# QK steps in groups of two across unit borders, PV in the spare PSUM banks, column-tiled sums from unit 3 on

## The chip, the cores and the metric

One core of a Trainium2 chip. The metric is device time in microseconds (us) of one execution. Engines: TensorE (PE in the profile, PEld its weight loads), VectorE (DVE), ScalarE (ACT), GpSimd (POOL), and SyncE (SP), which issues most DMAs. Runs were timed in several rounds; the kernel before was timed in each, and its median there was 436.7 to 437.2.

## The reference

Attention with RMS-normalised queries and keys (8 batches, 12 heads, 448 tokens, head size 64), then a two-layer MLP over all tokens (768 to 2048 to 768) with a leaky ReLU:

```python
q_n, k_n = rmsnorm(q, g_q), rmsnorm(k, g_k)
attn = softmax(q_n @ k_n.T / sqrt(64))          # with the row maximum taken off
x = (attn @ v).transpose(0, 2, 1, 3).reshape(3584, 768)
h = x @ w_in
out = maximum(0.01 * h, h) @ w_out
```

## The kernel before

Four heads of one batch are a **unit** `u` (24 units, three to a batch). A unit has seven QK **steps**; a step is four 64x64-tiled matmuls that fill one **slot** (two PSUM banks; there are two slots), and one exponential on ScalarE empties it. The other four banks rotate as `aux` among everything else. PV is the product of the exponentials with the values (28 tiled matmuls a unit), `zcol` the sums by which it is divided. A step's maximum over all its rows (VectorE), a diagonal `dg`, a broadcast matmul into `pb` and two short VectorE steps give the shift `eb` of the unit's exponentials. MLP work of the batch before is cut into jobs (`moe1`: 6 matmuls of 448 columns, evacuated by ScalarE; `moe2`: 8 matmuls of 384 columns, every second one evacuated by VectorE) and dealt out between the QK groups.

```python
STEPS = ((0,), (1, 2), (3, 4), (5, 6))          # four groups a unit

def fed(u, d):                                   # a batch is complete here
    return u % NQ == 0 and d == 3

def fill(u, d, jobs):                            # deals the queue out evenly up to the next feeding
    total = sum(c for c, _ in queue)
    ...                                          # left: the weights up to fed(...), unit 3 excluded
    debt[0] += total * WD[d] / left
    while queue and debt[0] >= queue[0][0] * 0.5:
        c, fn = queue.pop(0); fn(); debt[0] -= c
        if jobs: jobs.pop(0)()
    for job in jobs: job()
...
push_moe1(0); push_moe2(0)                       # prologue: batch 0 is queued here
...
for u in range(3, NU):
    for d in range(4):
        qk(u, STEPS[d])
        if d == 0:
            shift_max(u)
            pv_slot(u - 1); zcol(u - 1)          # PV takes the second slot
            shift_mm(u)
            pv_out(u - 1); zcol_sum(u - 1)
        ex(u)
        ...
        if fed(u, d) and u > 3:                  # not for unit 3: batch 0 is queued already
            push_moe1(u // NQ - 1); push_moe2(u // NQ - 1)
        ...
            if d == 1: ...job(prep_ssq, u + 2, ALL, (ti,))       # sums of squares
            if d == 2:
                job(prep_rinv, u + 2)
                for ti in range(2):                              # queries, then keys
                    job(prep_norm, u + 2, ALL, (ti,))            # VectorE, 1.1 us each
                job(prep_trd, u + 2)                             # DMA transpose
        fill(u, d, jobs)                         # d == 3 has no VectorE preparation
```

(shortened; `...` marks cuts)

## Time and profile before

| what | value | from |
|---|---|---|
| time | 436.72 us (436.13 to 436.79, 3 runs) | timed runs |
| TensorE busy, clock granted | 96%, 0.995 | page, run |
| ScalarE, VectorE, GpSimd busy | 71%, 49%, 34% | page |
| idle of TensorE from 100 to 390 us | 0 | table of stretches |

The profiled execution of this kernel took 438.52 us, 1.8 more than the median of the timed ones. The prediction below shows the chain and the stretches. First the groups of instructions for the two MLP layers (line, engine, operation, shapes, count, busy time and mean), which count the work:

```profile
L350 PE MATMUL op<-wout,gt 128*128 128x384 f16 x896 | 153.6, 326 | 0.0
L329 PE MATMUL hps<-xt,win 128*128 128x448 f16 x756 | 151.0, 353 | 0.0
```

896 is 112 second-layer jobs of 8, and 756 is 126 first-layer jobs of 6 (two more ran in the prologue): each batch once. Then VectorE around the start of a unit (start, length, what, idle before it in brackets):

```profile
209.32 1.09 DVE L151 TENSOR_TENSOR n<-qg,rinv 128x896 f16<-128x896 f32 x1 [6.96 <-issue]
210.33 1.08 DVE L151 TENSOR_TENSOR n<-rk,rinv 128x896 f16<-128x896 f32 x1
214.42 1.10 DVE L216 TENSOR_REDUCE sT<-sT 128x1 f32<-128x896 f32 x1 [3.01 <-PE sT L179]
```

The two normalising multiplications (L151) are done 3 us before the next unit's maximum (L216): VectorE waits for TensorE there, not the other way round. In the whole run TensorE waited 2.0 us for the diagonal.

### The profile page before, as it was taken

The page shows a single profiled execution, that of the slowest core. Times are in us where ns is not written, and L with a number is a line of the kernel's source. Part 1 is how long each engine was busy: PE and PEld are TensorE (multiplying, and loading weights), DVE is VectorE, ACT ScalarE, POOL GpSimd, SP SyncE. Part 2 cuts the span into 40 slices and gives each one's busy share as a digit, 9 for nine tenths or more (in the row PEclk, how much of TensorE's full clock was granted, in tenths as well). Part 3 has the DMA queues.
Part 4 walks back from the last instruction along what each step waited for, and adds up shares of the span by engine and source line. Part 5 has one row for each costly group of instructions (what it writes and reads, how often), then busy time and mean ns, then how long its engine had stood idle before and what let it go on. Part 6 is the DMA issues. An engine that isn't in the chain of part 4 may idle for free.

```text
span 436.7 us, 8782 instructions
## 1 busy us (share of the span) xinstructions
PE 419.2 (96%) x3700; PEld 216.3 (50%) x3700; DVE 214.8 (49%) x319; ACT 309.5 (71%) x458; POOL 148.9 (34%) x102
## 2 busy tenths in 40 slices
PE   7788998999999999999999999999999999999995
PEld 6545443444455544554445544554445544555563
DVE  5887564874535744554445745555345612220021
ACT  6989887688976699877876699867877486534300
POOL 4987566533422432532330422532430110100000
PEclk9989999999999999999999999999999999999999
DMA  8999999689458856569447875779524630311022
GB/s 276 220 257 249 235 189 192 182 198 208 91 143 144 216 152 125 129 200 204 85 128 146 203 177 102 148 205 184 108 44 107 134 75 2 78 38 38 0 74 72
DMA packets 67980, 62.83 MB, mean 144 GB/s; under 512 B 37477, under 2 KB 62821, under 8 KB 67941
## 3 DMA queue, kind: packets, MB, share of 16 engines
q1 hardware_dynamic: 57664, 50.47, 46.7%
q0 software_dynamic: 10272, 11.80, 17.6%
q8 instruction: 29, 0.48, 0.4%
q14 instruction: 11, 0.08, 0.1%
q10 hardware_dynamic: 4, 0.00, 0.0%
HBM read 45.61 MB, written 11.01 MB: 130 GB/s over the span
## 4 chain that ended last, share of the span: by engine, by line
PE 83%; ACT 6%; DVE 5%; DMA 3%; issue 1%; DVEq 0%; ACTq 0%
PE op L350 32%; PE hps L329 31%; PE sT L179 8%; PE sT L314 5%; ACT et L198 4%; DMA qkT<-n 3%; PE zc L260 3%; DVE n L151 2%; PE sT L243 1%; PE pb L228 1%; PE warm L412 1%; DVE ssq L139 1%; DVE sT L216 0%; ACT rz L301 0%; ACT rz L300 0%
## 5 line engine op out<-in xcount | busy, mean ns | idle before, releaser
L198 ACT ACTIVATE et<-sT,eb 128x896 f16<-128x896 f32 x166 | 158.8, 1005 | 47.8 <-PE sT L179 35.7
L350 PE MATMUL op<-wout,gt 128*128 128x384 f16 x896 | 153.6, 326 | 0.0
L329 PE MATMUL hps<-xt,win 128*128 128x448 f16 x756 | 151.0, 353 | 0.0
L350 PEld LDWEIGHTS <-gt 128*128 128x128 f16 x896 | 84.7, 98 | 65.3 <-issue 12.1
L329 PEld LDWEIGHTS <-win 128*128 128x128 f16 x756 | 70.9, 98 | 71.3 <-issue 7.2
L294 POOL TENSOR_TENSOR xt<-x,rz 128x896 f16<-128x896 f32 x19 | 41.0, 2156 | 185.9 <-DMA rz<-zs 170.6
L331 ACT ACTIVATE gt<-hps 128x448 f16<-128x448 f32 x126 | 67.7, 544 | 21.3 <-PE hps L329 20.2
L354 DVE COPY ost<-op 128x384 f32<-128x384 f32 x56 | 31.1, 556 | 99.4 <-PE op L350 96.2
L134 POOL TENSOR_TENSOR qg<-rq,ggb 128x896 f32<-128x896 f32 (+2 forms) x25 | 61.3, 2454 | 36.7 <-DVE n L151 32.3
L179 PE MATMUL sT<-qkT 64*64 64x448 f16 x664 | 52.2, 364 | 6.4 <-ACT et L198 4.3
L151 DVE TENSOR_TENSOR n<-qg,rinv 128x896 f16<-128x896 f32 (+2 forms) x25 | 27.5, 1102 | 54.3 <-issue 26.7
L139 DVE TENSOR_REDUCE ssq<-sq 128x14 f32<-128x896 f32 (+2 forms) x49 | 50.0, 1053 | 1.1 <-ACT sq L126 1.1
L216 DVE TENSOR_REDUCE sT<-sT 128x1 f32<-128x896 f32 x22 | 24.1, 1093 | 31.9 <-PE sT L179 31.7
L179 PEld LDWEIGHTS <-qkT 64*64 64x64 f16 x672 | 15.4, 104 | 40.3 <-issue 35.0
L151 DVE TENSOR_TENSOR n<-rk,rinv 128x896 f16<-128x896 f32 (+2 forms) x25 | 33.6, 1348 | 0.0
L272 ACT COPY x<-sT 128x896 f32<-128x896 f32 x19 | 17.2, 906 | 19.4 <-PE sT L314 19.4
L314 PE MATMUL sT<-et,vt 64*64 64x448 f16 x532 | 28.4, 349 | 0.0
L314 PEld LDWEIGHTS <-vt 64*64 64x64 f16 x672 | 19.8, 107 | 10.5
L106 POOL DMA_DIRECT2D vt<-in_v_dram x24 | 18.4, 765 | 0.0
L126 ACT ACTIVATE sq<-rq 128x896 f32<-128x896 f32 (+2 forms) x19 | 17.3, 913 | 1.2 <-DMA rq<-in_q_dram 1.2
L126 ACT ACTIVATE sq<-rk 128x896 f32<-128x896 f32 x17 | 16.2, 955 | 0.0
L260 PE MATMUL zc<-et,onesr 128*32 128x448 f16 (+1 forms) x304 | 16.1, 332 | 0.0
(64 smaller groups left out, 212.2 us busy)
## 6 DMA issues: line engine op xcount, KB each, us to landing
rq<-in_q_dram SPq DMA_DIRECT2D x24, 448.0 KB, 5.2
rk<-in_k_dram SPq DMA_DIRECT2D x24, 448.0 KB, 5.9
out_dram<-ost SPq DMA_DIRECT2D x56, 192.0 KB, 2.8
rz<-zs SPq DMA_DIRECT2D x38, 224.0 KB, 3.3
vt<-in_v_dram POOLq DMA_DIRECT2D x24, 224.0 KB, 5.0
win<-in_moe_w_in_dram POOLq DMA_DIRECT2D x8, 384.0 KB, 15.8
wout<-in_moe_w_out_dram POOLq DMA_DIRECT2D x2, 1536.0 KB, 27.2
qkT<-n SPq DMA_TRANSPOSE x19, 4.3
```

What stands on the lines that cost most here:

```text
L126: nc.scalar.activation(buf(u, "sq")[:, ti, :, c[0]:c[1]], raw[u][ti][:, :, c[0]:c[1]], AF.Square)
L134: eng.tensor_tensor(buf(u, "qg")[:, :, c[0]:c[1]], raw[u][0][:, :, c[0]:c[1]], ggb[:, None, None, :].broadcast_to([P, 2, n, D]), op=ALU.mult)
L139: nc.vector.tensor_reduce(buf(u, "ssq")[:, ti, :, c[0]:c[1]], buf(u, "sq")[:, ti, :, c[0]:c[1]], axis=AXL.X, op=ALU.add)
L151: nc.vector.tensor_tensor(buf(u, "n16")[:, ti, c[0]:c[1]].rearrange("p s a d -> p a s d"), src[:, :, c[0]:c[1]], buf(u, "rinv")[:, ti, :, ...
L179: nc.tensor.matmul(banks[a][64 * r:64 * r + 64, 0:S].rearrange("p (t x) -> p t x", t=NS), kT(u, r, a, t), qT(u, r, a), start=True, stop=True)
L198: nc.scalar.activation(s["et"][:, t], sT[:, :, 0:S], AF.Exp, bias=s["eb"], scale=1.0)
L294: nc.gpsimd.tensor_tensor(xts[b][:, g], s["x32"], s["rz"], op=ALU.mult)
L314: nc.tensor.matmul(s["pv"][r][64 * a:64 * a + 64, 0:S], vts[u % NV][64 * r:64 * r + 64, a, t], s["et"][64 * r:64 * r + 64, t, a], start=(t ...
L329: nc.tensor.matmul(hps[:, 0:S], win16[:, kt // 2, kt % 2, ts(ft, P)], xt[:, kt // 2, kt % 2], start=(kt == 0), stop=(kt == KT - 1))
L331: nc.scalar.activation(gt[:, ft, ds(S * (b % 2), S)], hps[:, 0:S], AF.Prelu, bias=0.0, scale=1.0, alpha=0.01)
L350: nc.tensor.matmul(op2[:, 0:HC], gt[:, ft, ts(t, P)], wout16[:, ft, ds(HC * half, HC)], start=(ft == 0), stop=(ft == FT - 1))
L354: nc.vector.tensor_copy(ost[0][:, ds(HC * half, HC)], op2[:, 0:HC])
```

## The change

The intent: the 14 QK steps of two units make seven groups of two, where there were four groups to each unit (1+2+2+2), so TensorE changes between full and tiled matmuls less often. PV no longer needs a slot; it takes two of the `aux` banks. Unit 3's column sums get the narrower form that later units had (`narrow`), and unit 5's queries and keys are transposed on TensorE instead of by DMA. The core of the diff, with the tail of the output as well:

```diff
-        nc.scalar.copy(s["x32"], s["pslot"][:, :, 0:S])
+        for r in range(2):
+            nc.scalar.copy(s["x32"][:, r], s["pv"][r][:, 0:S])
 ...                       # the last output tile: two engines copy, two queues send, each half at once
+            nc.vector.tensor_copy(ost[0][:, HC * half:HC * half + HC // 2], op2[:, 0:HC // 2])
+            nc.scalar.copy(ost[0][:, HC * half + HC // 2:HC * half + HC], op2[:, HC // 2:HC])
 ...
+    for u in range(4, NU, 2):
+        order = [(u, t) for t in range(NS)] + [(u + 1, t) for t in range(NS)]
+        for x in range(NS):
+            groups.append((order[2 * x:2 * x + 2], (2.9, 4.0, 4.0, 4.0, 2.9, 4.0, 4.0)[x]))
-    def fed(u, d):
-        return u % NQ == 0 and d == 3
+    def fed(gi):
+        if gi < FIRST:
+            return 0
+        y, x = divmod(gi - FIRST, NS)
+        u = 4 + 2 * y
+        if x == 3 and u % NQ == 0:
+            return u // NQ
+        if x == 0 and (u - 1) % NQ == 0:
+            return (u - 1) // NQ
+        return 0
 ...
+            if x == 0:                              # n = u + 1
+                shift_max(u); pv(u - 1); zcol(u - 1); shift_mm(u)
+                pv_out(u - 1); zcol_sum(u - 1); ex(u)
+                job(zcol_inv, u - 1); early(u)      # early: loads, GpSimd's scaled queries (u + 2)
+            elif x == 1: ex(u); xmul_pool(u - 1); sums_of_squares(u)
+            elif x == 2: ex(u); norms(u)
+            elif x == 3:
+                ex(u); shift_max(n)
+                job(lambda: None); job(shift_ex, n) # broadcast and first exponential of n
+                ...
+            elif x == 4: pv(u); zcol(u); pv_out(u); zcol_sum(u); ex(n); job(zcol_inv, u); early(n)
+            elif x == 5: ex(n); xmul_pool(u); sums_of_squares(n); ...
+            else: ex(n); norms(n); ...
-                if fed(u, d) and u > 3:
-                    push_moe1(u // NQ - 1)
-                    push_moe2(u // NQ - 1)
+            if fed(gi) > 0:
+                push_moe1(fed(gi) - 1)
+                push_moe2(fed(gi) - 1)
```

(several statements put on one line here)

More of the change, by code (lines that the diff above doesn't have):

```diff
@@ L182, in qk @@
     def qk(u, steps):
-        st[u]["sT"] = []
+        st[u].setdefault("sT", [])
         for t in steps:
@@ L198, in ex @@
                 nc.scalar.activation(s["et"][:, t], sT[:, :, 0:S], AF.Exp, bias=s["eb"], scale=1.0)
+        s["sT"] = []
     def score0(u):
@@ L261, in zcol @@
                                      start=(t < 2), stop=(t in (4, 5)))
-    def pv_slot(u):
-        s = st[u]
-        s["pslot"] = slot()
-        s["pv"] = [s["pslot"][:, r] for r in range(2)]
-        pv(u)
     def pv_out(u):
@@ L308, in pv @@
         s = st[u]
-        if t0 == 0 and "pslot" not in s:
+        if t0 == 0:
             s["pv"] = [aux([P, 512], FP32, "pv") for r in range(2)]
@@ L342, in moe2 @@
     def moe2(pair, t, half, part):
+        last = pair == B // 2 - 1 and t == NS - 1
         if half == 0 and part == 0:
@@ L353, in moe2 @@
             return
-        nc.vector.tensor_copy(ost[0][:, ds(HC * half, HC)], op2[:, 0:HC])
-        if half == 1:
+        if last:
+            nc.vector.tensor_copy(ost[0][:, HC * half:HC * half + HC // 2], op2[:, 0:HC // 2])
+            nc.scalar.copy(ost[0][:, HC * half + HC // 2:HC * half + HC], op2[:, HC // 2:HC])
+        else:
+            nc.vector.tensor_copy(ost[0][:, ds(HC * half, HC)], op2[:, 0:HC])
+        if half == 1 or last:
+            c = slice(HC * half, HC * half + HC) if last else slice(0, DM)
             for y in range(2):
@@ L359, in moe2 @@
                 dst = out[b * S:(b + 1) * S, :].rearrange("(p t) m -> p t m", t=NS)
-                nc.sync.dma_start(dst[:, grp, :], ost[0][64 * y:64 * y + 64, :])
+                eng = nc.scalar if last and y else nc.sync
+                eng.dma_start(dst[:, grp, c], ost[0][64 * y:64 * y + 64, c])
     queue = []
@@ L372, in push_moe2, with fill @@
                     queue.append((1.31, lambda b=b, t=t, half=half, part=part: moe2(b // 2, t, half, part)))
-    WD = (3.6, 2.9, 2.8, 2.8)
     STEPS = ((0,), (1, 2), (3, 4), (5, 6))
     debt = [0.0]
-    def narrow(u):
-        return 4 <= u < NU - 1
-    def fed(u, d):
-        return u % NQ == 0 and d == 3
-    def fill(u, d, jobs):
-        total = sum(c for c, _ in queue)
-        left = WD[d] + 3.0
-        uu, dd = u, d
-        while True:
-            dd += 1
-            if dd == 4:
-                uu, dd = uu + 1, 0
-            if uu == NU or (fed(uu, dd) and (u > 3 or uu > 3)):
+    groups = [((), 3.6)] + [([(3, t) for t in STEPS[d]], 2.9) for d in range(1, 4)]
+    FIRST = len(groups)
+    for u in range(4, NU, 2):
+        order = [(u, t) for t in range(NS)] + [(u + 1, t) for t in range(NS)]
+        for x in range(NS):
+            groups.append((order[2 * x:2 * x + 2], (2.9, 4.0, 4.0, 4.0, 2.9, 4.0, 4.0)[x]))
+    def narrow(u):
+        return 3 <= u < NU - 1
+    def fed(gi):
[8 more added lines that the diff above has]
+        return 0
+    def fill(gi, jobs):
+        total = sum(c for c, _ in queue)
+        w = groups[gi][1]
+        left = w + 3.0
+        for gj in range(gi + 1, len(groups)):
+            if fed(gj) > 0:
                 break
-            left += WD[dd]
-        debt[0] += total * WD[d] / left
+            left += groups[gj][1]
+        debt[0] += total * w / left
         while queue and debt[0] >= queue[0][0] * 0.5:
@@ L588 @@
         del queue[0:2]
-        for u in range(3, NU):
-            for d in range(4):
-                if d > 0 or u > 3:
-                    qk(u, STEPS[d])
-                    if d == 0:
-                        shift_max(u)
-                        if narrow(u - 1):
-                            pv_slot(u - 1)
-                            zcol(u - 1)
-                            shift_mm(u)
-                            pv_out(u - 1)
-                            zcol_sum(u - 1)
-                        else:
-                            zsum_slot(u - 1)
-                            pv(u - 1)
-                            shift_mm(u)
-                            zinv(u - 1)
-                    ex(u)
-                jobs = []
-                def job(fn, *args):
-                    jobs.append(lambda: fn(*args))
-                if d == 0:
-                    if u == 3:
-                        prep_norm(4)
-                        gate(4)
-                    elif narrow(u - 1):
-                        job(zcol_inv, u - 1)
-                    else:
-                        xmul(u - 1)
-                    if u + 4 < NU:
-                        job(load, u + 4)
-                    if u + 2 < NU:
-                        prep_qg(u + 2, nc.gpsimd)
-                    if u + 3 < NU:
-                        load_v(u + 3)
-                    if u < 6:
-                        prep_sqp(u + 3)
-                if d == 1 and u > 3 and narrow(u - 1):
-                    xmul_pool(u - 1)
-                if fed(u, d) and u > 3:
-                    push_moe1(u // NQ - 1)
-                    push_moe2(u // NQ - 1)
-                if u == 3 and d == 1:
@@ new lines, in early, with sums_of_squares, norms @@
+        def early(u):
+            if u + 4 < NU:
+                job(load, u + 4)
+            if u + 2 < NU:
+                prep_qg(u + 2, nc.gpsimd)
+            if u + 3 < NU:
+                load_v(u + 3)
+            if u < 6:
+                prep_sqp(u + 3)
+        def sums_of_squares(u):
+            if u + 2 < NU:
+                for ti in range(2):
+                    job(prep_ssq, u + 2, ALL, (ti,))
+        def norms(u):
+            if u + 2 < NU:
+                job(prep_rinv, u + 2)
+                for ti in range(2):
+                    job(prep_norm, u + 2, ALL, (ti,))
+                if u > 3:
+                    job(prep_trd, u + 2)
@@ new lines, in squares, with shift_ex, job @@
+        def squares(u, ti):
+            if 6 <= u < NU - 3:
+                job(prep_sq, u + 3, ALL, (ti,))
+        def shift_ex(u):
+            shift_mm(u)
+            ex(u)
+        for gi, (steps, w) in enumerate(groups):
+            jobs = []
+            def job(fn, *args):
+                jobs.append(lambda: fn(*args))
+            for u, t in steps:
+                qk(u, (t,))
+            if gi < FIRST:
+                if gi > 0:
+                    ex(3)
+                if gi == 0:
+                    prep_norm(4)
+                    gate(4)
+                    early(3)
+                elif gi == 1:
@@ L635 @@
                     for ti in range(2):
                         prep_tr(4, ti, VV)
-                if u + 2 < NU:
-                    if d == 1:
-                        for ti in range(2):
-                            job(prep_ssq, u + 2, ALL, (ti,))
-                    if d == 2:
-                        job(prep_rinv, u + 2)
-                        for ti in range(2):
-                            job(prep_norm, u + 2, ALL, (ti,))
-                        job(prep_trd, u + 2)
-                if d == 3 and 6 <= u < NU - 3:
-                    for ti in range(2):
-                        job(prep_sq, u + 3, ALL, (ti,))
@@ L649 @@
-                fill(u, d, jobs)
+                    sums_of_squares(3)
+                elif gi == 2:
+                    norms(3)
+                fill(gi, jobs)
+                continue
+            y, x = divmod(gi - FIRST, NS)
+            u = 4 + 2 * y
+            n = u + 1
+            if x == 0:
+                shift_max(u)
+                pv(u - 1)
+                zcol(u - 1)
+                shift_mm(u)
+                pv_out(u - 1)
+                zcol_sum(u - 1)
+                ex(u)
+                job(zcol_inv, u - 1)
+                early(u)
+                if u == 4:
+                    for ti in range(2):
+                        prep_tr(5, ti, VV)
+            elif x == 1:
+                ex(u)
+                xmul_pool(u - 1)
+                sums_of_squares(u)
+            elif x == 2:
+                ex(u)
+                norms(u)
+            elif x == 3:
+                ex(u)
+                shift_max(n)
+                job(lambda: None)
+                job(shift_ex, n)
+                for ti in range(2):
+                    squares(u, ti)
+            elif x == 4:
+                pv(u)
+                zcol(u)
+                pv_out(u)
+                zcol_sum(u)
+                ex(n)
+                job(zcol_inv, u)
+                early(n)
+            elif x == 5:
+                ex(n)
+                xmul_pool(u)
+                sums_of_squares(n)
+                squares(n, 0)
+            else:
+                ex(n)
+                norms(n)
+                squares(n, 1)
@@ L650 @@
+            if fed(gi) > 0:
+                push_moe1(fed(gi) - 1)
+                push_moe2(fed(gi) - 1)
+            fill(gi, jobs)
         zsum_slot(NU - 1)
```

## The prediction

> **What bounds the kernel now.** I read the page first (busy time, slices, chain), then the chain in order of time for one attention unit in the middle, then the waits, then the timeline of TensorE at both ends. First the page: which engine, and over what part of the span.
>
> ```profile
> PE 419.2 (96%) x3700; PEld 216.3 (50%) x3700; DVE 214.8 (49%) x319; ACT 309.5 (71%) x458; POOL 148.9 (34%) x102
> ...
> PE   7788998999999999999999999999999999999995
> ...
> PE 83%; ACT 6%; DVE 5%; DMA 3%; issue 1%; DVEq 0%; ACTq 0%
> ```
>
> TensorE is the bound, from the seventh slice (about 70 us) to the last. A busy matmul row alone does not say that it streams at full rate, so I take start-to-start times from the chain in order of time (start, length, what). One unit between two pairs of banks:
>
> ```profile
> 206.46 3.51 PE hps L329 x18
> 209.97 0.50 PE sT L179 x8
> 210.47 3.51 PE hps L329 x18
> 213.98 0.31 PE sT L179 x4
> 214.30 1.32 PE sT L314 x28
> 215.62 0.78 PE zc L260 x16
> 216.40 0.16 PE pb L228
> 216.56 3.40 PE hps L329 x18
> ```
>
> 18 dense matmuls that follow another full-array matmul take 3.40 us, 189 ns each; after a QK group the same 18 take 3.51. A QK group of 8 takes 0.50 us. Four tiles run at once, so its streaming is 2 x 189 = 378 ns. So each visit to the small tiles costs 0.12 + 0.11 = 0.23 us above its work. Nothing else is between the pieces: TensorE is saturated by matmul work plus these visits. The table of stretches says the same of 100 to 390 us:
>
> ```profile
> 100.00:390.00 290.00, 290.00 (x2484) 143.03 (x2477) 137.67 (x203) 220.55 (x325) 82.37 (x46) 1.00 0.60 134
> ```
>
> (length, then TensorE matmul, weight load, DVE, ACT, POOL busy, granted clock, DMA.) What idle time TensorE has in the part that the change touches is at the passage from prologue to steady state (timeline of TensorE, idle in brackets):
>
> ```profile
> 53.30 0.38 PE L179 MATMUL sT<-qkT 64*64 64x448 f16 x4 [0.37 <-ACT et L198]
> ...
> 66.76 0.38 PE L179 MATMUL sT<-qkT 64*64 64x448 f16 x4 [0.37 <-ACT et L198]
> ...
> 70.88 0.38 PE L179 MATMUL sT<-qkT 64*64 64x448 f16 x4 [1.36 <-DMA qkT<-n]
> ...
> 86.68 0.22 PE L228 MATMUL pb<-dg,onesp 128*128 128x128 f16 x1 [0.82 <-DVE dg L218]
> ```
>
> The end, from the chain and the timeline, gives the clean price of the two MLP jobs and the drain:
>
> ```profile
> 392.72 18.16 PE hps L329 x96
> 410.88 20.81 PE op L350 x128
> 431.72 0.56 DVE ost L354
> ...
> 432.30 1.11 SPq L360 DMA_DIRECT2D out_dram<-ost  x2
> ```
>
> 96 first-layer matmuls (16 jobs of 6) take 18.16 us, 1.135 us a job; 128 second-layer matmuls (16 jobs of 8) take 20.81 us, 1.30 us a job. From the last copy's end (432.28) to the end of the span (436.7) are 4.4 us of output transfer.
>
> **What the Trainium skill says.** "TensorE: Matmul & The Clock Gate", section "Wait — 56ns, not 53.3ns?": a warm matmul of N columns starts every N / 2.4 GHz plus about 2.5 ns. For 448 columns that is 189.2 ns and for 384 162.5; the trace has 18.16 / 96 = 189.2 and 20.81 / 128 = 162.6. So each added dense matmul has a price that nothing can hide on a full TensorE. "TensorEngine Tiling (Array Packing)", section "Key Properties": changing the tiling mode drains the TensorE. The trace agrees in kind, with 0.23 us for the two changes of a visit. "Perfetto Trace Analysis", section "Optimizing Tensor Performance": independent matmul groups should rotate through different PSUM banks so that evacuation overlaps. The change moves PV into the same four rotating banks that the MLP uses; before, those never stalled in 100 to 390 us.
>
> **The change part by part.**
>
> 1. Grouping. Units 4 to 23 visit the small tiles 4 times each, 80 visits; now 7 for two units, 70. 10 x 0.23 = **-2.3 us**. The QK matmuls themselves stay at 672.
>
> 2. PV in the spare banks and column sums of unit 3. PV costs the same on TensorE (28 matmuls, 1.32 us). Its evacuation becomes two ACT copies of 448 columns in place of one of 896 (0.906 us); by the 0.54 us of the ACT row of the same size each, overlapped a little, about 0.1 us more per unit on an engine that is 71% busy: off the path. Unit 3's 28 summing matmuls (1.32 to 1.45 us) become 16 (0.78): -0.5. Unit 5's keys and queries are turned on TensorE instead of by DMA: 14 transposes, which took 0.79 us in unit 3 (47.64 to 48.43): +0.8. Together **+0.3 us**.
>
> 3. The idle above. The 1.36 us wait for the DMA transpose goes (unit 5 no longer uses it, and unit 3 gets longer); of the two ACT waits, the DVE wait and two QK groups stretched from 0.50 to 0.80 us at 78 and 91 us, more work between groups should cover about half. **-2.6 us** in all.
>
> 4. The end. The last copy is split over two engines (half of 0.56, plus fixed cost: about -0.2) and the two last transfers are issued by two queues side by side instead of one after the other (half of 1.11), of half the size: **-0.9 us**.
>
> 5. The part that the summary does not mention. The function that says when a batch is complete was rewritten. Before, it excluded unit 3, because the prologue has already queued batch 0. Now, for the first pair (u = 4, first group) it computes (4 - 1) / 3 = 1 and returns 1, which is above zero, so the main loop queues the first and second layer of batch 0 **again**. The prologue's own two calls are untouched by the diff. The results are the same numbers written a second time, so no check of correctness sees it. The extra work: 16 first-layer jobs (96 matmuls), 18.16 us, and 12 second-layer jobs (3 output tiles x 2 halves x 2 parts, 96 matmuls), 96 x 162.6 ns = 15.61 us. Sum **+33.8 us** of TensorE. Stepping the queue's bookkeeping by hand: the first copy of batch 0 is nearly used up within unit 3 (7, 5, 5 and 4 jobs in its four groups), because the same function also ends the stretch over which the queue is spread; the second copy then feeds units 4 to 6 at the usual 3 or so jobs a group. Before, one copy was spread over units 3 to 6. TensorE had only some 3 us idle there in 50 us, so nearly nothing of the 33.8 is absorbed beyond point 3.
>
> 6. New waits. The group that ends one unit and starts the next has the next unit's first scores in the second slot. That slot is freed only after maximum (1.09), diagonal (0.29), broadcast matmul behind the second MLP job, two short DVE steps (0.46) and the exponential (1.01), about 4.6 to 4.9 us after the group began; the next group's second QK step wants it at about 0.6 + 3 x 1.2 + 0.25 = 4.5. Up to 0.3 us, ten times: **+3 us**, the least certain term.
>
> Sum: 436.7 - 2.3 + 0.3 - 2.6 - 0.9 + 33.8 + 3 = **468 us**; as I may have been hard on point 6, I say 467.
>
> **Rivals.**
>
> A. The intent alone: the batch is not really queued twice, or the repeat hides. Then 436.7 - 2.3 + 0.3 - 2.6 - 0.9 + 0 to 3 = 431 to 434, within 2%. For it: an author who timed this would have seen a loss. Against: the code path is short and has no guard, and slices full of nines leave no room to hide 192 matmuls.
>
> B. ACT becomes the bound in the first-layer stretches. At 200 to 220 us it idles only 2.3 us. The repeat adds 16 ACT evacuations of 0.54 us, and the boundary group may carry two squares of 0.95 besides two exponentials. If ACT falls behind, the four rotating banks fill and TensorE waits for them: 0.5 us in each of some 20 groups, 475 us or more. Against: the second-layer stretches leave ACT free to catch up, since DVE evacuates there.
>
> C. The second-layer weights are not there when unit 3's denser filling asks for them. They are issued at 33.4 and 35.1 us and take 23.9 and 30.5 us to land, so until 57 to 66 us. The new order wants them at about 63 us, ten before. A wait of 0 to 2 us, once.
>
> D. PV in the rotating banks stalls the first MLP job after it, until ACT has copied. PV ends 0.8 us before that job, and one copy takes 0.54: covered, unless ACT is late (then B).
>
> **Range and chances.** The repeat is arithmetic from the diff and fixed prices: 33.8 with an error under 1. The other terms sum to between -7 and +4: 463 to 474 at the extremes, so **462 to 472** for 8 in 10, point 467. Faster by over 2% needs me to be wrong about the repeat and low on the rest: 0.01. Within 2% (to 445.4): 0.03. Slower: 0.96.
>
> **What would show each step.** Repeat: the first-layer dense matmuls go from 756 to 852, the second-layer ones from 896 to 992, ACT's first-layer evacuations from 126 to 142, output transfers from 56 to 64 (6 repeated, 2 from the split), and all TensorE matmuls from 3700 to about 3894. Grouping: QK groups of 8 everywhere after unit 3, still 0.50 us each, and a chain of TensorE pieces without gaps. Point 3: no wait of TensorE for the DMA transpose. Point 6: the wait of the QK matmuls for the exponentials, 4.3 us in 11 waits before, grows to about 7. Rival B: waits of the dense matmuls for ACT's evacuations, absent before. Wrong altogether: unchanged matmul counts.

## The result, and the profile after

| | before | after |
|---|---|---|
| time, us | 436.75 (436.13 to 437.23, 4 runs) | 484.02 (481.7 to 485.64, 4 runs) |
| ratio | | 1.108 (95%: 1.103 to 1.113), slower |
| TensorE matmuls | 3700 | 3894 |

Ratios are the mean time of one kernel's fast runs over that of the other's fast runs of the same rounds, so not quite the ratio of the medians quoted. The direction was foretold; the size, 467 with a range of 462 to 472, was not: 17 us are missing. The page of the changed kernel:

```profile
PE 455.1 (94%) x3894; PEld 238.6 (49%) x3894; DVE 216.3 (45%) x327; ACT 317.0 (66%) x497; POOL 147.8 (31%) x103
...
PE   7778999999999989979999989979999999999996
...
PEclk9999999999999999998999999999999999999999
...
PE 61%; DVE 13%; ACT 12%; DMA 6%; issue 4%; POOL 3%; SPq 1%; POOLq 0%; ACTq 0%; DVEq 0%
```

Three things to see. TensorE's busy time grew by 36 us. Its row of nines now has holes in the middle (an 8 and, three slices on, a 7, and the same again nine slices later), where before there were none from the eighth slice on, and one slice of the clock row has a dent beside a hole. And the chain that ended last, 83% TensorE and 5% VectorE before, is now 61% and 13%. The groups of the two layers (L347 and L325 are what L350 and L329 were):

```profile
L347 PE MATMUL op<-wout,gt 128*128 128x384 f16 x992 | 171.5, 330 | 0.0
L325 PE MATMUL hps<-xt,win 128*128 128x448 f16 x852 | 169.1, 353 | 0.0
```

96 more of each: batch 0 is computed twice, as foretold. The waits of TensorE in the whole run (total us, times, longest):

```profile
PE pb L229 <- DVE dg L219: 14.2, 14, 2.9
PE sT L179 <- ACT et L198: 5.1, 13, 0.9
```

The wait for the diagonal went from 2.0 to 14.2 us. The timeline at the start of a pair of units (all engines, lines left out):

```profile
211.63 1.09 DVE L151 TENSOR_TENSOR n<-qg,rinv 128x896 f16<-128x896 f32 x1 [8.41 <-issue]
...
212.64 0.55 DVE L355 COPY ost<-op 128x384 f32<-128x384 f32 x1
212.80 2.09 POOL L134 TENSOR_TENSOR qg<-rq,ggb 128x896 f32<-128x896 f32 x1 [2.63 <-DVE n L151]
213.11 2.73 DVE L151 TENSOR_TENSOR n<-rk,rinv 128x896 f16<-128x896 f32 x1
...
213.53 0.85 PE L261 MATMUL zc<-et,onesr 128*32 128x448 f16 x16
...
215.76 1.08 DVE L217 TENSOR_REDUCE sT<-sT 128x1 f32<-128x896 f32 x1
...
216.88 0.29 DVE L219 TENSOR_TENSOR dg<-ident,sT 128x128 f16<-128x128 f16 x1
217.22 0.22 PE L229 MATMUL pb<-dg,onesp 128*128 128x128 f16 x1 [2.84 <-DVE dg L219]
...
217.28 4.13 PE L347 MATMUL op<-wout,gt 128*128 128x384 f16 x16
```

The scores whose maximum is wanted were ready by 212.1 us, after the QK group that began at 211.71. But the maximum (L217) starts at 215.76, because VectorE first does the two multiplications that the group before left in its queue, and the second of these takes 2.73 us while GpSimd multiplies beside it. TensorE gets to the broadcast at 214.4 and stands for 2.84 us. Then the 16 second-layer matmuls after the wait take 4.06 us to the next group (217.28 to 221.34), against 2.71 elsewhere. The table of stretches shows why (the last columns are granted clock, DMA share, GB/s):

```profile
217.00:221.40 4.40, 4.18 (x21) 1.96 (x24) 1.87 (x5) 2.94 (x4) 0.00 (x0) 0.67 0.84 141
```

A granted clock of 0.67: after an idle of 2.8 us, the matmuls behind it cost another 1.35 us. The same happens once more, after the wait of 2.92 us that ends at 324.5 us (16 matmuls in 4.26).

### The profile page after: what moved, and what is told of

Same layout as the page of the kernel before. It is cut to its first block, busy times and chain, and to the rows that moved or that the text cites. A ratio compares the mean times of both kernels' runs of the same rounds, so it can differ in the third digit from the quotient of the medians.

```text
span 483.9 us, 9230 instructions
## 1 busy us (share of the span) xinstructions
PE 455.1 (94%) x3894; PEld 238.6 (49%) x3894; DVE 216.3 (45%) x327; ACT 317.0 (66%) x497; POOL 147.8 (31%) x103
## 4 chain that ended last, share of the span: by engine, by line
PE 61%; DVE 13%; ACT 12%; DMA 6%; issue 4%; POOL 3%; SPq 1%; POOLq 0%; ACTq 0%; DVEq 0%
PE op L347 30%; PE hps L325 21%; DVE n L151 6%; PE sT L179 5%; ACT et L198 5%; DMA rz<-zs 5%; DVE sT L217 3%; POOL xt L290 3%; PE pv L310 2%; DMA rq<-in_q_dram 1%; ACT sq L126 1%; ACT x L268 1%; ACT gt L327 1%; DVE ost L355 1%; DVE dg L219 1%
## 5 line engine op out<-in xcount | busy, mean ns | idle before, releaser
L347 PE MATMUL op<-wout,gt 128*128 128x384 f16 x992 | 171.5, 330 | 0.0
L325 PE MATMUL hps<-xt,win 128*128 128x448 f16 x852 | 169.1, 353 | 0.0
L347 PEld LDWEIGHTS <-gt 128*128 128x128 f16 x992 | 95.2, 99 | 80.6 <-issue 21.9
L325 PEld LDWEIGHTS <-win 128*128 128x128 f16 x852 | 80.1, 98 | 83.9 <-issue 12.3
L327 ACT ACTIVATE gt<-hps 128x448 f16<-128x448 f32 x142 | 74.5, 540 | 30.6 <-PE hps L325 30.4
L355 DVE COPY ost<-op 128x384 f32<-128x384 f32 x60 | 33.4, 556 | 110.5 <-PE op L347 107.7
L310 PE MATMUL pv<-et,vt 64*64 64x448 f16 x672 | 36.6, 349 | 0.0
L268 ACT COPY x<-pv 128x448 f32<-128x448 f32 x40 | 19.3, 536 | 24.0 <-PE pv L310 23.8
L217 DVE TENSOR_REDUCE sT<-sT 128x1 f32<-128x896 f32 x22 | 24.0, 1092 | 14.9 <-ACT gt L327 12.6
L273 DVE COPY zs<-zc 64x448 f32<-64x448 f32 x20 | 12.5, 626 | 35.2 <-PE zc L261 34.9
L229 PE MATMUL pb<-dg,onesp 128*128 128x128 f16 x24 | 5.4, 223 | 14.3 <-DVE dg L219 14.2
## 6 DMA issues: line engine op xcount, KB each, us to landing
out_dram<-ost SPq DMA_DIRECT2D x60, 192.0 KB, 3.4
```

The costliest lines, as they stand in the source:

```text
L217: nc.vector.tensor_reduce(s["spare"][:, 511:512], sT[:, :, 0:S], axis=AXL.XY, op=ALU.max)
L310: nc.tensor.matmul(s["pv"][r][64 * a:64 * a + 64, 0:S], vts[u % NV][64 * r:64 * r + 64, a, t], s["et"][64 * r:64 * r + 64, t, a], start=(t ...
L325: nc.tensor.matmul(hps[:, 0:S], win16[:, kt // 2, kt % 2, ts(ft, P)], xt[:, kt // 2, kt % 2], start=(kt == 0), stop=(kt == KT - 1))
L327: nc.scalar.activation(gt[:, ft, ds(S * (b % 2), S)], hps[:, 0:S], AF.Prelu, bias=0.0, scale=1.0, alpha=0.01)
L347: nc.tensor.matmul(op2[:, 0:HC], gt[:, ft, ts(t, P)], wout16[:, ft, ds(HC * half, HC)], start=(ft == 0), stop=(ft == FT - 1))
L355: nc.vector.tensor_copy(ost[0][:, ds(HC * half, HC)], op2[:, 0:HC])
```

## The experiments

Theories before the first runs. **Theory 1**: the repeat costs its work on TensorE, some 31 to 34 us, and most of the rest is the VectorE queue ahead of the maximum. **Theory 2**: all comes from the repeat, through crowding of ScalarE, VectorE or DMA. **Rival 3**: PV in the rotating banks, or a late ScalarE, makes the stalls.

**e1_once.** The changed kernel, batch 0 queued once:

```diff
-        if x == 0 and (u - 1) % NQ == 0:
+        if x == 0 and u > 4 and (u - 1) % NQ == 0:
```

> The changed kernel with batch 0 queued once (the completeness function no longer fires for unit 3), everything else as changed. Theory 1 (the repeat costs its TensorE work, 33.8 us, and the rest of the loss is a wait of the broadcast matmul for VectorE at the start of a pair): 484 - 33.8 = 450 us, so still slower than before by about 13, with 12 to 14 us of TensorE waiting for the diagonal. Theory 2 (all of the loss comes from the repeat, directly or by crowding other engines): 431 to 436 us and no such waits. Matmul counts 756 and 896 in both.

Measured: 461.45 us (459.61 to 464.35), 1.057 of before. Theory 2 falls: without the repeat there are still 25 us too many. But taking the repeat out gave back 22.6, not 33.8, so theory 1 missed by 11 us; TensorE's waits for the diagonal between 44 and 440 us even grew, from 12.7 to 17.6 us. e4 and e5 find where.

**e2_before_twice.** The kernel before with the repeat alone:

```diff
-                if fed(u, d) and u > 3:
+                if fed(u, d):
```

> The kernel before, with batch 0 queued a second time at the end of unit 3 and nothing else changed. Theory 1: 436.7 + 33.8 less 2 to 3 us of idle filled = 467 to 471 us, no waits of TensorE for the diagonal beyond the 2 us there were. Theory 2 (the repeat carries the whole 47 us): 480 us or more.

Measured: 468.05 us (467.98 to 468.71), 1.072: 31.2 us more, close to 33.8 less the idle time that it fills (in the traces, TensorE's idle from 44 to 130 us falls from 3.5 to 0.6 us). The wait for the diagonal stays small:

```profile
PE pb L228 <- DVE dg L218: 1.6, 3, 0.6
```

The repeat by itself causes no stalls.

**e3_norms_early.** The changed kernel with the repeat, the second unit's sums and normalisation one group earlier:

```diff
             elif x == 4:   ...  early(n)
+                sums_of_squares(n)
             elif x == 5:
-                sums_of_squares(n)
+                norms(n)
             else:
-                norms(n)
```

> The changed kernel, repeat kept, with the sums of squares and the normalising multiplications for the second unit of a pair moved one group earlier (fifth and sixth group in place of sixth and seventh), so that VectorE has no such work queued right ahead of the next pair's maximum. Theory 1: the 12.7 us of waits for the diagonal between 100 and 440 us and the 2.7 us of half-rate clock after the two longest go nearly all: 468 to 471 us. Rival 3 (the stall comes from PV sharing the rotating banks, or from ScalarE being late): no change, 482 to 486.

Measured: 470.4 us (470.08 to 470.5), 13.6 less than the changed kernel, as theory 1 said. The wait for the diagonal, which was 14.2 us:

```profile
PE pb L229 <- DVE dg L219: 3.3, 5, 1.1
```

Rival 3 falls: PV still sits in the rotating banks, and the same ScalarE work is there.

**e4_once_early.** The edits of e1 and e3 together.

> Both edits together: batch 0 once and the normalisation one group earlier. Theory 1: 484 - 33.8 - 14 = 434 to 437 us, so about equal to the kernel before or up to 3 us faster: what the grouping was meant to give. Theory 2 and rival 3 give the same time as the run with batch 0 once.

Measured: 447.52 us (444.56 to 449.83), 1.025 of before: 10.5 us above the upper end of what was expected. After 106 us TensorE idles at most 1.1 us in 50; the larger loss lies before. TensorE at unit 5's start:

```profile
72.10 0.23 PE L229 MATMUL pb<-dg,onesp 128*128 128x128 f16 x1 [3.31 <-DVE dg L219]
...
73.96 0.49 PE L179 MATMUL sT<-qkT 64*64 64x448 f16 x4 [1.31 <-ACT et L198]
74.17 2.89 PE L310 MATMUL pv<-et,vt 64*64 64x448 f16 x28
```

In units 3 to 6 the one copy of batch 0 must last for 14 groups, so a group is 3 to 4 us long, and the first unit's multiplications (third group) run into the second unit's maximum (fourth group) as well. PV then takes 2.89 us instead of 1.49, the granted clock being 0.76 to 0.81 from 72 to 80 us. With the repeat, longer groups covered this (no wait for the diagonal between 44 and 140 us in the changed kernel): so removing the repeat gives back less than its work.

**e5_once_both_early.** As e4, and the first unit's sums and normalisation also one group earlier:

```diff
             if x == 0:     ...  early(u)
+                sums_of_squares(u)
             elif x == 1:
-                sums_of_squares(u)
+                norms(u)
             elif x == 2:
-                norms(u)
```

> The run with batch 0 once and the second unit's normalisation early (447.5 us), with the first unit's sums and normalisation moved one group earlier too (first and second group instead of second and third), so that the maximum in the fourth group also has no multiplications queued right ahead of it. If the 10 us that this run still lacks at 58 to 106 us are the same VectorE queue wait, now in the thinly filled units 4 to 6 (waits of 3.3 and 2.5 us and the half-rate clock after them): 437 to 441 us. If they are something else about a thin filling (exponentials too late): 446 to 448.

Measured: 439.12 us (438.94 to 441.13), 1.005 of before. The waits for the diagonal between 44 and 440 us are down from 7.7 to 0.9 us, so most of e4's loss was the same VectorE queue. Not all: from 44 to 106 us TensorE still idles 4.3 us, of which 3.3 are six waits for an exponential (the longest 1.31, at 71 us). The changed kernel, with the repeat, has none of these before 129 us, so the thin filling leaves them; no run with batch 0 once removes them.

**e6_keys_first.** The changed kernel, repeat and place kept, the keys multiplied before the queries:

```diff
                 job(prep_rinv, u + 2)
-                for ti in range(2):
+                for ti in (1, 0):
                     job(prep_norm, u + 2, ALL, (ti,))
```

> The changed kernel, repeat kept, normalisation in its place, but the keys multiplied before the queries. The buffer of scaled queries then comes free only after both multiplications, so that GpSimd's next multiplication cannot run beside the second of them, which took 2.0 to 2.7 us with it and 1.1 without. If this running side by side makes a good part of the wait: 1 to 1.6 us less at some six pair starts and no half-rate clock, 472 to 478 us. If only the place in the queue matters: 481 to 485.

Measured: 475.15 us (474.76 to 475.86), 8.9 less than the changed kernel. VectorE's groups for the multiplications, keys and queries, first in the changed kernel, then here (busy us, mean ns after the bar):

```profile
L151 DVE TENSOR_TENSOR n<-rk,rinv 128x896 f16<-128x896 f32 x23 | 31.9, 1387 | 0.0
L151 DVE TENSOR_TENSOR n<-qg,rinv 128x896 f16<-128x896 f32 x23 | 25.2, 1095 | 68.8 <-POOL xt L290 28.4 <-issue 21.6 <-ACT rinv L145 18.8
```

```profile
L151 DVE TENSOR_TENSOR n<-rk,rinv 128x896 f16<-128x896 f32 x23 | 25.1, 1090 | 66.8 <-ACT rinv L145 66.8
L151 DVE TENSOR_TENSOR n<-qg,rinv 128x896 f16<-128x896 f32 x23 | 25.0, 1088 | 0.7 <-ACT rinv L145 0.7
```

The mean of the second multiplication falls from 1387 to 1088 ns; in the worst cases it was 2.73 us. GpSimd waits for the single buffer of scaled queries. When the queries went first, that buffer came free between the two multiplications and GpSimd ran beside the second. Which of the two begins first matters: in every stretched case of the changed kernel between 100 and 440 us (177.7, 212.6, 230.7, 285.6, 319.9 and 337.9 us), an output copy on VectorE (L355) stands between the two multiplications, so that GpSimd begins before the second; where they follow each other directly, VectorE takes its 1.08 us and GpSimd 2.86 instead of 2.08 (193.1 us, for one). The kernel before has both cases too. The Trainium skill, "SBUF — State Buffer", section "Who interferes with whom", says that a VectorE instruction with two SBUF inputs contends with a GpSimd instruction that reads SBUF; these rows agree. The longest wait for the diagonal between 100 and 440 us is now 1.2 us, and the clock stays at 1.00 in every stretch there, although output copies still stand between some of the multiplications. So the place in the queue makes the stall (in e3 it nearly goes), and GpSimd's beginning ahead of the second multiplication made it long.

**e7_once_both_early_keys_first.** e5 and e6 together.

> Batch 0 once, both normalisations early, keys first: everything found so far mended. Theory: 433 to 437 us; the grouping's 2.3 us and the end's 0.6 us should show against the kernel before, so 433.5 if nothing is left.

Measured: 440.26 us (438.7 to 442.77), 1.008 (1.005 to 1.011). Missed: nothing gained over e5, and the kernel before is not beaten. In steady state, between PV starts six units apart in the timelines, the kernel before takes 99.14 us (131.73 to 230.87) and this one 99.81 (132.51 to 232.32). Three visits fewer should give 0.7 back (3 x 0.23). They are eaten where the pair's second unit comes in:

```profile
196.16 0.22 PE L229 MATMUL pb<-dg,onesp 128*128 128x128 f16 x1
...
198.47 0.38 PE L179 MATMUL sT<-qkT 64*64 64x448 f16 x4 [0.64 <-ACT et L198]
```

The wait for the slot splits a QK group: from the group's beginning (197.44) to PV (198.65) are 1.21 us, where a group ahead of PV takes 0.40 elsewhere. The other groups of this kind in the six units are stretched less, one to 0.65 us (131.86 to 132.51). Both come again 100 us later (231.68, 297.25). Together 1.1 us are lost in six units for the 0.7 won; the last 0.3 of the difference I did not trace. Ahead of that, from 44 to 106 us, e7 keeps the waits that e5 left: TensorE idles 3.7 us, 3.3 of it for exponentials, where the kernel before idles 3.5, 1.36 of it the DMA wait that only some of its runs have. The two profiles differ less than the medians: spans of 437.2 us here, in one of the faster runs, and 436.7 for before, in a slow one. The timed runs scatter up to 442.8, and what the slower of them pay no profile shows.

**e8_before_tail.** The kernel before with only the change's output end (the hunk of the last output tile).

> The kernel before with the split of the last output alone. The changed kernel's trace has 4.4 us from TensorE's last matmul to the end against 5.0 before: 0.5 to 0.9 us faster, 436.0.

Measured: 435.66 us (435.44 to 436.4), 0.9966 (0.9949 to 0.9983). The profiled run had no wait for unit 5's DMA transpose, which had cost 1.36 us in the profiled run of before. That wait comes in some runs: e12's profile has it (1.9 us), e11's does not. So part of a difference between single runs is luck.

**e9_before_mended.** e8 with unit 5 turned on TensorE and keys first:

```diff
-                        job(prep_trd, u + 2)
+                        if u > 3:
+                            job(prep_trd, u + 2)
+                if u == 4 and d == 0:
+                    for ti in range(2):
+                        prep_tr(5, ti, VV)
```

> The kernel before (units of four groups, PV in a slot, one queueing of each batch) with the parts of the change that cost nothing: the split end, unit 5 turned on TensorE in place of the DMA transpose, and the keys normalised before the queries. Expected: 0.6 from the end, up to 1.4 from the DMA wait that came in some runs, 0.8 from the wait for the diagonal at 87 us, less 0.8 for the transposes: 434.5 to 436, and less scatter between runs than before. If the end is all that counts: the same as with the end alone, 435.7.

Measured: 436.94 us (436.77 to 437.28), 1.0005. A miss: a cause is argued here, not tested. The runs agree more closely, but 14 transposes and a new wait of 0.24 us stand against a DMA wait that only some runs pay (in two of the four profiles of such kernels), and the wait at 87 us stayed (0.77).

**e10_shift_first.** e7 with the broadcast after the first job:

```diff
-                job(lambda: None)
                 job(shift_ex, n)
```

> The run with everything mended (440.3 us), with the broadcast matmul and the first exponential of the pair's second unit placed after the first MLP job of the fourth group in place of the second. The prediction's point 6 (the slot is held until that exponential, so the next QK step waits) would then lose its wait, 0.64 us once in 100 us and some 0.2 to 0.3 us elsewhere that lie inside stretched QK rows: 438 to 439.5 us. If TensorE now waits for the diagonal in its place (about 0.3 us at each of ten): 440 to 442.

Measured: 440.59 us (439.66 to 442.23), 1.0097: no gain, by the second of the two ways named.

```profile
195.68 0.22 PE L229 MATMUL pb<-dg,onesp 128*128 128x128 f16 x1 [0.19 <-DVE dg L219]
...
198.27 0.57 PE L179 MATMUL sT<-qkT 64*64 64x448 f16 x8
```

The wait for the slot is gone and the broadcast waits instead, at each of these places. The chain of maximum, diagonal, broadcast and exponential is as long as the group; in the two orders tried, its wait was moved and not removed.

**e11_tail_again** and **e12_tail_keys.** e8 once more, and e8 with the keys first.

> The kernel before with the split end alone, a second time, because the run with it and two more edits came out no faster than before. If the end's gain is real: 0.6 to 1.5 us below the kernel before again. If the first result was luck of the chip: equal.

> The split end and the keys normalised first, unit 5 turned by DMA as before. If the 14 transposes on TensorE (0.8 us) were what gave the end's gain back in the earlier run: as fast as the split end alone, or up to 0.8 us faster (the wait for the diagonal at 87 us). If the order of the two multiplications costs something here: slower than the split end alone.

Measured: 436.41 us, 0.9979 (0.9958 to 0.9999), and 435.85 us, 0.9974 (0.9954 to 0.9993). The split end is worth 0.2 to 0.3%, twice seen; the order of the multiplications adds nothing measurable to it. The kernels of e8 (run again as e11) and e12 are the fastest of the study and beat both kernels of the case, by a margin well under 2%.

## Why the prediction was wrong in size

The 47.3 us divide along the runs: 31.2 from before to e2, 2.4 from e2 to e3, 13.6 from e3 to the changed kernel.

- **Point 5, the repeat: right.** Counts to the instruction (852, 992, 3894). Its price of 33.8, less the 2.9 us of idle that e2's trace lacks against that of before (3.5 and 0.6), is 30.9; measured were 31.2.
- **Point 3, idle covered: right while the repeat is there, with some luck.** Foretold were 2.6 us (the parts as listed add up to 2.4); e2's trace covers 2.9, the changed kernel's somewhat more (0.3 us idle from 44 to 92, against 3.5). But 1.36 of it is a DMA wait read from one slow execution of before, which e8's and e11's profiles do not have. Without the repeat it does not hold (e4, e5).
- **Point 2, PV and sums: too small to test.** The two copies take 0.97 us for 0.91, the 14 transposes of unit 5 took 0.77.
- **Point 1, grouping: the mechanism stands, no gain was seen.** Groups of eight QK matmuls still cost 0.50 us between MLP jobs, and there are fewer of them. But e3 is 2.4 us slower than e2, where points 1, 2, 4 and 6 added up to 0. TensorE idles 3.6 us in e3's trace from 44 to 425 us and 0.6 in e2's, so waits of about the +3 of point 6 are left once the queue is mended (1.8 for the diagonal, 1.4 for exponentials); what takes the remaining 2 us is not shown.
- **Point 4, the end: 0.6 for 0.9.** From TensorE's last matmul to the end of the span there are 4.4 us for 5.0. The two copies of the last half were meant to run side by side and ran one after the other:

```profile
479.53 0.36 DVE L352 COPY ost<-op 128x192 f32<-128x192 f32 x1 [2.24 <-PE op L347]
479.92 0.32 ACT L353 COPY ost<-op 128x192 f32<-128x192 f32 x1 [2.28 <-DMA out_dram<-ost]
```

- **Point 6, new waits: this step failed.** It gave +3 us, from "maximum (1.09), diagonal (0.29), broadcast matmul behind the second MLP job", counted from the group's beginning, as if VectorE were free then. It was not: the changed order puts the normalisation in the group directly ahead of the next pair's maximum, where the kernel before had one group between them. The prediction looked only at the maximum in the middle of the pair and at the slot; that wait for ScalarE came to 1.4 us between 44 and 440 us (over the whole run 5.1, where about 7 were foretold). The wait for the diagonal, mostly at the pair's start, came to 12.7 there, and two spells at a lower clock added 1.35 and 1.55. Moving the normalisation alone (e3) gave 13.6 us back, against the +3 of this term; waits of 3.2 us remained.
- **Rivals.** A (no repeat) and D fall by the traces. B is not borne out: nowhere between 44 and 440 us does a dense matmul of the changed kernel wait for ScalarE. C did not come: the second-layer jobs of unit 3 run without a wait at 62.5 to 72.3 us.

Three slips in the text change nothing: ScalarE idles 2.0 us from 200 to 220, not 2.3; the range of 462 to 472 begins below the 463 that it calls an extreme, and the nines of TensorE's row are unbroken from the eighth slice on (76 us), not the seventh.

What stays open: the 2 us between e2 and e3 named above; the stretched rows in e7, which show no releaser, so their cause was not tested; and why the timed runs of the changed kernel, e1, e4, e5 and e7 scatter by 2 to 5 us, where those of the kernel before scatter by 1 to 3.

## What to carry to other kernels

When a schedule is regrouped, go through every in-order engine's queue, not only the one that bounds: list what stands directly ahead of each short instruction that the bounding engine waits for, and keep one group of distance. When a condition is rewritten, evaluate it by hand at its first and last index; a repeat that writes the same numbers passed the check of correctness here, and the instruction counts of the profile showed it. And price a saving together with the latency chain of its new place: seven groups for eight should have won some 0.7 us in six units, and 1.1 were lost to the chain.

## What the Trainium skill lacked or had wrong

- "TensorE: Matmul & The Clock Gate", section "What's actually happening", gives an idle window of about 3.4 us for the half-rate clock. Here shorter waits were followed by it: after 2.84 us the granted clock was 0.67 over the next 4.4 us, and 16 matmuls took 4.06 us for 2.71; after 2.45 us in e4 (at 104.0) it was 0.60 over 4 us. It is not certain, either: in e1, one wait of 2.93 us (to 192.0) left the clock at 1.00, the 16 matmuls behind it taking 2.69 us, and another of 2.93 (to 297.6) was followed by 16 in 5.25 us. Waits of 1.3 us in the changed kernel brought no such spell.
- "TensorEngine Tiling (Array Packing)", section "Key Properties", names the drain on a change of tiling mode without a figure. Here the two changes of one visit cost 0.23 us.
- "SBUF — State Buffer", section "Who interferes with whom", has the contention of VectorE and GpSimd, and that the order of issue decides, but no measured time for this pair. In the changed kernel the VectorE multiplication of 128x896 took 1.09 us alone and 2.73 when GpSimd's had begun 0.31 us before it (212.80 and 213.11), and GpSimd's took 2.08 alone (mean in e6) and up to 2.87 when VectorE's had begun first.
